# Two cached-attention blocks on one core: the V rows of every fourth pack, their P times V tiles, and where TensorE's loop begins

## The chip, the cores and the metric

The kernel runs on one core of a Trainium2 chip. The metric is the device time of one execution in microseconds (us); lower is better. Of the kernel before there are three timed runs, 747.2, 747.67 and 748.57 us, with a median of 747.67 us, and one profiled execution.

## The reference

Two independent blocks, A and B, each compute the same thing on their own inputs, and the two outputs are joined along the last axis. B is the batch here, H the heads.

```python
B, Sq, D = x.shape            # 16, 64, 640
H, Dh = 32, 128               # k_cache, v_cache: (16, 32, 512, 128), all bf16
q = (x @ wq).reshape(B, Sq, H, Dh).transpose(0, 2, 1, 3)
scores = einsum("bhqd,bhkd->bhqk", q, k_cache) * Dh ** -0.5
p = softmax(scores, axis=-1)
o = einsum("bhqk,bhkd->bhqd", p, v_cache)
return o.transpose(0, 2, 1, 3).reshape(B, Sq, H * Dh) @ wo
```

K and V of both blocks are 268 MB in all, and each byte of them is used once.

## The kernel before

**Packs, turns, phases.** The work is cut into 128 packs, numbered n. A pack is four heads of two batch rows: its K is 1 MB, its V is 1 MB. Four packs (j = n % 4) that share the same two batch rows make a turn, eight turns (all 16 batch rows) make a phase, and there are four phases: the two halves of the heads of block A, then those of block B. A phase has its own quarter of the weights: `wq` through `ws_sb` into `wqp_sb`, and `wo` into `wo_sb`.

**What is done for a pack.** Names are those of the emitters, line numbers those of the profile of before.

- `LDK` (L556, issued by SP): four DMAs of 256 KB into `kn_ring`, six packs deep, in rows of 8 KB.
- `LDV` (L567 or L569, SP): two DMAs of 512 KB into `v_ring`, four packs deep. The load of pack n waits until P times V of pack n - 4 is done.
- `KT` (L621, DVE): the 32 x 32 transposes of K into `kt_ring`, twice per pack.
- `QP` (L607, PE): 20 matmuls for q. `QE` (L613, ACT): q to `qs_ring`.
- `S` (L631, PE): 32 matmuls, the scores into four PSUM banks.
- `EX` (L650, ACT): four exponentials with row sums. `RC` (L663, DVE): reciprocals. `NM` (L679, POOL): four multiplications, P normalised, into `pn_sb`.
- `TR` (L690, PE): 32 transposes of P. `TE` (L700, DVE): two copies to `pT_sb`.
- `PV` (L714, PE): P times V. `OE` (L722, ACT): two copies of the result to `oT_sb`; `ZO` (L726, ACT): a piece of PSUM set to zero.
- `OP` (L734, PE): 8 matmuls with `wo`. After the fourth pack of a turn, `OS` (L744 or L747, DVE) adds to `acc` or `out_sb`, and in phases 1 and 3 `ST` (L753) stores.
- `XT` (L586, PE), once per turn: transposes of x.

**Wide and narrow packs.** There are two layouts of V. In a wide pack a partition of `v_ring` holds 16 consecutive key positions of one head: the DMA moves 128 rows of 4 KB, head i lies in partitions 32 i to 32 i + 31, and `PV` is 128 matmuls on tiles of 32 rows, four such tiles (one per head) next to each other in the array. In a narrow pack a partition holds 8 key positions of each of two heads: the DMA moves 256 rows of 2 KB, and `PV` is 64 matmuls on tiles of 64 rows, two next to each other. `EX` and `NM` lay out P to suit, with the same number of instructions and elements. Before, the packs with j = 0, 1 or 2 are wide and those with j = 3 are narrow (`WIDE = (0, 1, 2)`): 96 wide packs and 32 narrow ones.

**The order of the work.** The table `AT` gives each operation of pack n a due time in units of packs, and each engine runs its list in order of due time. So PE runs, again and again: `QP(n)`, `PV(n-2)`, `S(n)`, `TR(n-1)`, `OP(n-2)`, and once in four packs `XT`. SP's list holds the K and V loads (and some of the weights) in due order; ACT, beside its arithmetic, issues the other weight loads and the stores. Semaphores carry the dependencies.

**TensorE's loop.** All engines but PE run their lists written out. On PE one turn is emitted once, as the body of a loop (L813) that runs 32 times; the pieces ahead of it (one `XT`) and behind it (`PV(126)`, `TR(127)`, `OP(126)`, `PV(127)`, `OP(127)`) are written out. Every matmul is two instructions, a load of the stationary operand (PEld) and the matmul itself; with 821 matmuls, 13 separate waits, 7 subtractions from semaphores and 2 instructions of the loop itself, the body has 1664 instructions. A second, more general version of the program stands behind this one, and is run only if a row sum is out of range; it is not run here.

Of the kernel before, what the change touches and what calls it, by code (L numbers as in the profile page):

```python
# [20 lines left out]
class Cfg:  # L21
# [8 lines left out]
    PERIOD = 4  # L30
    BASE = 32
    KLEAD = 2.5
    WIDE = (0, 1, 2)
    AT = dict(XT=-2.585, XE=-2.383, XC=-0.788, QP=-0.428, QE=-0.224, KT=(-0.672, -0.375), S=0,
              EX=(0.252, 0.307, 0.358, 0.616), RC=(0.572, 0.794), NM=(0.803, 0.854, 1.088, 1.187),
              NMZ=(0.615, 1.231, 1.718, 1.794), TR=1.293, TE=(1.432, 1.47), PV=1.701, OE=(1.888, 2.013), ZO=2.221,
# [396 lines left out]
def mha_kernel(nc, blocks, out, cfg=None):  # L433
    cfg = cfg or Cfg()
# [7 lines left out]
    NBP, NJ = B // 2, 4  # L442
# [2 lines left out]
    assert H % HPH == 0 and NSUB == 2 and cfg.PERIOD == NJ and cfg.NV == NJ  # L445
    NPH = NBLK * NSUB
    NH = NBLK * NBP * H
    WIDE = cfg.WIDE

    plans = []  # L450
    for general in (False, True):
# [5 lines left out]
    with contextlib.ExitStack() as es:  # L457
# [42 lines left out]
        def pack_info(n):  # L500
            g, j = n // NJ, n % NJ
            ph = g // NBP
            return ph // NSUB, g % NBP, j, ph % NSUB * HPH + 4 * j
# [55 lines left out]
        def em_LDV(e, op):  # L559
            n, b = op.idx  # L560
            if n < 0:
                return None, None
            blk, bp, j, h = pack_info(n)
            src = blocks[blk][2][2 * bp + b, h:h + 4]
            dst = v_ring[:, n % NV, b]
            if j in WIDE:
                ins = e.dma_start(dst.rearrange("p t d -> p (t d)"), src.rearrange("h (p t) d -> (h p) (t d)", t=16))  # L567
            else:
                ins = e.dma_start(dst.rearrange("p (a t) d -> p a (t d)", a=2),  # L569
                                  src.rearrange("(a s) (p t) d -> (s p) a (t d)", s=2, t=8))  # L570
            return ins, ins
# [69 lines left out]

        def exp_views(h):
            src, dst = ps[:, h % 4, :], p_ring[:, h % NP, :]
            u = 2 if h // 4 % NJ in WIDE else 4
            return (src.rearrange("q (u t p) -> q t p u", u=u, p=16), dst.rearrange("q (t p u) -> q t p u", p=16, u=u))

        def em_EX(e, op):
            h = op.idx
            src, dst = exp_views(h)
            ins = e.activation(dst, src, ACTF.Exp, scale=1.0, accum_out=rowsum[:, h:h + 1])  # L650
            return ins, ins

        def em_EXG(e, op):
            h = op.idx
            r = h % 4
            src, dst = exp_views(h)
            ins = e.activation(dst, src, ACTF.Exp, bias=negmax[:, r:r + 1], scale=1.0, accum_out=rowsum[:, h:h + 1])
            return ins, ins
# [7 lines left out]
        def em_NM(e, op):  # L666
            h = op.idx
            i = h % 4
            if h < 0:
                ins = e.memset(pn_sb[:, :, :].rearrange("p t c -> p (t c)"), 0.0)  # L670
                return ins, ins
            if h // 4 % NJ in WIDE:
                dst = pn_sb[:, :, 32 * i:32 * i + 32]
                src = p_ring[:, h % NP, :].rearrange("q (t k) -> q t k", t=16)
            else:
                a, s = i // 2, i % 2
                dst = pn_sb[:, 8 * a:8 * a + 8, 64 * s:64 * s + 64]
                src = p_ring[:, h % NP, :].rearrange("q (t k) -> q t k", t=8)
            ins = e.tensor_scalar(dst, src, recip[:, h // 4 % NR, i:i + 1], 1.0, ALU.mult, ALU.mult)  # L679
            return ins, ins  # L680
# [21 lines left out]

        def em_PV(e, op):
            n = op.idx
            wide = n % NJ in WIDE
            tall, tiles, per = (32, 4, 16) if wide else (64, 2, 8)
            first = last = None
            for a in range(4 // tiles):
                for b in range(2):
                    for t in range(per):  # L710
                        for s in range(tiles):
                            rows = slice(tall * s, tall * s + tall)
                            i, c = a * tiles + s, a * per + t
                            last = e.matmul(ps[:, 4 + i, 64 * b:64 * b + 64], v_ring[rows, n % NV, b, c, :],  # L714
                                            pT_sb[rows, b, c, :], start=(t == 0 and i < 2), stop=(t == per - 1),
                                            tile_position=(tall * s, 0), skip_group_check=i >= 2)
                            first = first or last
            return first, last
# [60 lines left out]
        def units(key):  # L779
            return 16 if key[0].startswith("d_") else 1  # L780

        def emit(e, op, p, taken):
            sem = sems[p]
            waits = [(s, v - taken.get(s, 0)) for s, v in op.waits]
            attach = None
            if waits and not op.dma and op.kind not in ("FL1", "WP"):
                attach = waits.pop()
            for s, v in waits:
                e.wait_ge(sem[s], v * units(s))
            kind = "EXG" if p and op.kind == "EX" else op.kind  # L790
            first, last = emitters[kind](e, op)
            if last is None:
                e.sem_inc(sem[op.sem], units(op.sem))
                return
            if attach is not None:
                s, v = attach
                first.wait_op(sem[s], v * units(s), "sem-ge")
            last.then_inc(sem[op.sem], 16 if op.dma else 1)

        def run_program(e, eng, p):  # L800
            progs, counts, loop = plans[p]
            prog = progs[eng]
            if eng != "pe":
                for op in prog:
                    emit(e, op, p, {})
                return
            lo, size, reps, per = loop["lo"], loop["size"], loop["reps"], loop["per"]
            for key in sorted(counts):
                if key[0].startswith("q_"):
                    e.sem_inc(sems[p][key], cfg.BASE)  # L810
            for op in prog[:lo]:
                emit(e, op, p, {})
            with e.Fori(0, reps):  # L813
                taken = {}
                for i, op in enumerate(prog[lo:lo + size]):
                    emit(e, op, p, taken)
                    for s, v in sorted(per.items(), key=str):
                        if loop["take"][s] == i:
                            e.sem_inc(sems[p][s], -v * units(s))
                            taken[s] = v  # L820
            taken = {s: v * reps for s, v in per.items()}
            for op in prog[lo + size * reps:]:
                emit(e, op, p, taken)
# [7 lines left out]
        def run(e, eng):  # L831
            run_program(e, eng, 0)
            e.wait_ge(sems[0][("s_flc_dve",)], 1)
            with e.register("flag_" + eng) as r:
                e.reg_load(r, flag[0:1, 0:1])
                with e.If_ne(r, 128):
                    all_done(e, 0)
                    run_program(e, eng, 1)
                    if eng == "act":
                        all_done(e, 1, ("d_out",))  # L840
            if eng == "act":
                all_done(e, 0, ("d_out",))
# [22 lines left out]
def bass_concat_heads__mha_block_cached__mha_block_cached__near_ridge_kernel(  # L865
    nc: bass.Bass,
    A_x: bass.AP,
    A_k_cache: bass.AP,
    A_v_cache: bass.AP,
    A_wq: bass.AP,  # L870
    A_wo: bass.AP,
    B_x: bass.AP,
    B_k_cache: bass.AP,
    B_v_cache: bass.AP,
    B_wq: bass.AP,
    B_wo: bass.AP,
    out: bass.AP,
):
    blocks = [
        (A_x, A_k_cache, A_v_cache, A_wq, A_wo),  # L880
        (B_x, B_k_cache, B_v_cache, B_wq, B_wo),
    ]
    mha_kernel(nc, blocks, out, Cfg())
# [28 lines left out]
```

## Time and profile before

| | |
|---|---|
| timed runs, us | 747.2, 747.67, 748.57 (median 747.67) |
| profiled execution: span, us | 747.1 |
| what lies around the span | the profile gives no other time of this execution; the median is 0.57 us above its span |
| PE matmul, busy share | 681.3 us, 91% |
| PE weight load | 530.5 us, 71% |
| DVE, ACT, POOL busy | 514.9, 519.7, 404.0 us (69%, 70%, 54%) |
| DMA | 87518 packets, 295.15 MB, mean 395 GB/s |
| mean granted TensorE clock | 0.985 |

The span runs from the first to the last instruction. The engines' shares are averages over stages with different limits. "PE" is the matmul, "PEld" the load of the stationary operand, which overlaps it; SPq is the queue of DMA issues on SP. The DMA share in the tables by window is the time that packets took, divided by the time of 16 DMA engines; it can be over 1, because packets of one engine overlap a little.

### The profile page before, as it was taken

Reading aid. Unit: us, or ns where it says so; the run is one execution under the profiler, and the core shown is the slowest. Engines: PE = TensorE matmul, PEld = TensorE weight load, DVE = VectorE, ACT = ScalarE, POOL = GpSimd, SP = SyncE. Lnnn points to the kernel's source line nnn. Section 1 sums busy time; section 2 is a strip of 40 time slices with the busy share of each in tenths; the row PEclk is TensorE's granted clock in tenths of the full one; section 3 lists DMA queues with packets and bytes.
Section 4 is the critical chain, followed back from the end, with each engine's and each line's share of the span. In section 5 each row is a group of like instructions: output and inputs, shape, how many; then the busy total and the mean of one; then the engine's idle time right before and its main releaser. Section 6 shows DMA issues by size and latency. Waiting matters only on the chain.

```text
span 747.1 us, 57746 instructions
## 1 busy us (share of the span) xinstructions
PE 681.3 (91%) x26518; PEld 530.5 (71%) x26518; DVE 514.9 (69%) x818; ACT 519.7 (70%) x1559; POOL 404.0 (54%) x580
## 2 busy tenths in 40 slices
PE   2779999999999999999988999999997999999994
PEld 2557777777777777777766777777775777777773
DVE  6437777777777677676755676677676677877773
ACT  1438787787777677766756777777775677777772
POOL 3635555655965545545674455455486555555550
PEclk9879999999999999999999999999999999999998
DMA  9999999999999999999999999999999999999970
GB/s 326 391 402 411 412 411 414 411 410 413 405 400 415 411 414 411 412 413 414 410 400 406 410 413 413 412 410 410 413 407 402 410 413 413 413 414 411 410 301 17
DMA packets 87518, 295.15 MB, mean 395 GB/s; under 512 B 13360, under 2 KB 28208, under 8 KB 71088
## 3 DMA queue, kind: packets, MB, share of 16 engines
q1 hardware_dynamic: 76064, 281.43, 94.1%
q10 hardware_dynamic: 11408, 13.27, 5.0%
q14 instruction: 37, 0.30, 0.1%
q8 instruction: 9, 0.15, 0.1%
HBM read 292.03 MB, written 2.62 MB: 394 GB/s over the span
## 4 chain that ended last, share of the span: by engine, by line
SPq 35%; PE 30%; DMA 19%; POOL 5%; issue 4%; ACT 3%; DVE 3%; ACTq 0%; DVEq 0%
SPq L556 23%; PE ps L714 8%; DMA kn_ring<-in_A_k_cache_dram 8%; PE ps L734 7%; PE ps L607 6%; SPq L567 6%; DMA v_ring<-in_B_v_cache_dram 5%; SPq L569 5%; PE ps L631 4%; DMA kn_ring<-in_B_k_cache_dram 4%; PE ps L690 4%; POOL pn_sb L679 4%; DMA ws_sb<-in_A_wq_dram 2%; ACT p_ring L650 2%; ACT oT_sb L722 1%
## 5 line engine op out<-in xcount | busy, mean ns | idle before, releaser
L679 POOL TENSOR_SCALAR pn_sb<-p_ring,recip 128x512 bf16<-128x512 bf16 x508 | 341.8, 692 | 305.5 <-DVE recip L663 305.4
L621 DVE STREAM_TRANSPOSE kt_ring<-kn_ring 128x1024 f32<-128x1024 f32 x256 | 313.5, 1230 | 146.1 <-DMA kn_ring<-in_B_k_cache_dram 103.9
L650 ACT ACTIVATE p_ring<-ps 128x512 bf16<-128x512 f32 x512 | 298.9, 598 | 28.7 <-DMA xn_ring<-in_B_x_dram 6.7
L700 DVE COPY pT_sb<-ps 128x1024 bf16<-128x1024 bf16 x258 | 163.6, 674 | 71.6 <-PE ps L690 68.5
L714 PE MATMUL ps<-pT_sb,v_ring 32*128 32x64 bf16 (+1 forms) x14528 | 163.8, 192 | 26.1 <-DMA v_ring<-in_B_v_cache_dram 11.7
L714 PEld LDWEIGHTS ps<-pT_sb,v_ring 32*128 32x128 bf16 (+1 forms) x14528 | 146.6, 92 | 43.0 <-DMA v_ring<-in_B_v_cache_dram 14.5
L607 PE MATMUL ps<-xT_ring,wqp_sb 128*128 128x128 bf16 x2560 | 166.6, 221 | 7.6 <-POOL xT_ring L596 7.3
L734 PE MATMUL ps<-wo_sb,oT_sb 128*128 128x320 bf16 x1040 | 166.6, 303 | 3.3 <-issue 2.3
L607 PEld LDWEIGHTS ps<-xT_ring,wqp_sb 128*128 128x128 bf16 x2560 | 158.0, 114 | 14.7 <-issue 7.5
L722 ACT ACTIVATE oT_sb<-ps 128x256 bf16<-128x256 f32 x260 | 85.6, 381 | 116.7 <-PE ps L714 116.7
L631 PE MATMUL ps<-kt_ring,qs_ring 32*64 32x512 bf16 x4096 | 139.5, 384 | 0.0
L690 PEld LDWEIGHTS ps<-ident,pn_sb 64*128 64x128 bf16 x4128 | 69.9, 95 | 76.4 <-ACT ps L726 38.4
L613 ACT ACTIVATE qs_ring<-ps 128x512 bf16<-128x512 f32 x128 | 76.5, 598 | 66.6 <-PE ps L607 66.4
L734 PEld LDWEIGHTS ps<-wo_sb,oT_sb 128*128 128x128 bf16 x1040 | 91.9, 98 | 40.9 <-issue 2.5
L650 ACT ACTIVATION_READ_ACCUMULATOR p_ring<-ps 128x1 f32 x512 | 106.0, 207 | 0.0
L690 PE MATMUL ps<-ident,pn_sb 64*128 64x64 bf16 x4128 | 83.8, 191 | 19.6 <-POOL pn_sb L679 9.1
L631 PEld LDWEIGHTS ps<-kt_ring,qs_ring 32*64 32x64 bf16 x4096 | 53.3, 104 | 29.2 <-issue 1.4
L726 ACT ACTIVATE ps<-zeros 128x256 f32<-128x256 bf16 x130 | 51.3, 394 | 0.0
L579 POOL COPY wqp_sb<-ws_sb 128x1280 bf16<-128x1280 bf16 x32 | 39.2, 1255 | 16.4 <-DMA ws_sb<-in_A_wq_dram 16.4
L663 DVE RECIPROCAL recip<-rowsum 128x3 f32<-128x3 f32 (+1 forms) x256 | 36.9, 144 | 3.9 <-ACT p_ring L650 0.6
L596 POOL COPY xT_ring<-xs_sb 128x640 bf16<-128x640 bf16 x32 | 22.9, 716 | 2.0 <-PE ps L607 2.0
L586 PE MATMUL ps<-ident,xn_ring 128*128 128x128 bf16 x165 | 14.9, 222 | 3.3 <-DMA xn_ring<-in_A_x_dram 3.3
(26 smaller groups left out, 65.7 us busy)
## 6 DMA issues: line engine op xcount, KB each, us to landing
kn_ring<-in_A_k_cache_dram SPq DMA_DIRECT2D x256, 256.0 KB
v_ring<-in_A_v_cache_dram SPq DMA_DIRECT2D x128, 512.0 KB, 12.4
kn_ring<-in_B_k_cache_dram SPq DMA_DIRECT2D x256, 256.0 KB
v_ring<-in_B_v_cache_dram SPq DMA_DIRECT2D x128, 512.0 KB, 13.3
ws_sb<-in_B_wq_dram SPq DMA_DIRECT2D x10, 512.0 KB, 16.3
wo_sb<-in_B_wo_dram ACTq DMA_DIRECT2D x8, 640.0 KB, 12.4
ws_sb<-in_A_wq_dram ACTq DMA_DIRECT2D x4, 640.0 KB, 17.4
wo_sb<-in_A_wo_dram SPq DMA_DIRECT2D x4, 640.0 KB, 14.1
```

The costliest lines, as they stand in the source:

```text
L556: ins = e.dma_start(kn_ring[2 * b + l::4, n % NK].rearrange("p a c -> p (a c)"), src)
L607: last = e.matmul(ps[:, 1, f * 128:(f + 1) * 128], w[:, kt, f, :], xT_ring[:, xs, kt, :], start=(kt == 0), stop=(kt == KT - 1))
L613: ins = e.activation(qs_ring[:, op.idx % NQ].rearrange("p f b q -> p (f b q)"), ps[:, 1, :], ACTF.Copy, scale=scale)
L621: ins = e.transpose(dst.rearrange("p c b (h l) -> p c h b l", h=8, l=2), src)
L631: last = e.matmul(ps[64 * b:64 * b + 64, i, :], qs_ring[rows, n % NQ, f, b, :], kt_ring[rows, n % NKT, :, f // 2, b, :, f % 2], start=(f = ...
L650: ins = e.activation(dst, src, ACTF.Exp, scale=1.0, accum_out=rowsum[:, h:h + 1])
L679: ins = e.tensor_scalar(dst, src, recip[:, h // 4 % NR, i:i + 1], 1.0, ALU.mult, ALU.mult)
L690: last = e.transpose(pt_bank(b)[:, 64 * c:64 * c + 64], pn_sb[rows, c, :], ident[rows, rows], tile_position=(64 * b, 0))
L700: ins = e.tensor_copy(pT_sb[:, b].rearrange("p t q -> p (t q)"), pt_bank(b))
L714: last = e.matmul(ps[:, 4 + i, 64 * b:64 * b + 64], v_ring[rows, n % NV, b, c, :], pT_sb[rows, b, c, :], start=(t == 0 and i < 2), stop=(t ...
L722: ins = e.activation(oT_sb[:, 2 * a:2 * a + 2, :], o_ps[:, 2 * a:2 * a + 2, :], ACTF.Copy)
L734: last = e.matmul(out_ps[:, s, :], oT_sb[:, i, :], wo_sb[:, 4 * j + i, s * NH0:(s + 1) * NH0], start=(j == 0 and i == 0), stop=(j == NJ - ...
```

## The change

A pack is now wide unless it is one of the last two: `wide(n)` is true for n below 126. So 126 packs are wide and 2 (126 and 127) narrow: thirty-one packs go from narrow to wide, and pack 126 goes from wide to narrow. The same test picks the layout in the load of V, in `EX`, `NM` and `PV`. The body of TensorE's loop gets 64 more matmuls and so 128 more instructions, 1792 in all. The loop is now made on PE alone with `nc.Fori(..., head_slot={e.engine: 0})`: the loader is asked to place the loop's first instruction at instruction slot 0 of a fetch block of 256 instructions, with a branch over the slots left unused ahead of it. The lists of SP, ACT, DVE and POOL, with their waits, are the same.

```diff
-    WIDE = (0, 1, 2)
+    NARROW = 2
...
-    WIDE = cfg.WIDE
+    NPACK = NH // 4
+
+    def wide(n):
+        return n < NPACK - cfg.NARROW
...
-            if j in WIDE:
+            if wide(n):
                 ins = e.dma_start(dst.rearrange("p t d -> p (t d)"), src.rearrange("h (p t) d -> (h p) (t d)", t=16))
...
-            u = 2 if h // 4 % NJ in WIDE else 4
+            u = 2 if wide(h // 4) else 4
...
-            if h // 4 % NJ in WIDE:
+            if wide(h // 4):
                 dst = pn_sb[:, :, 32 * i:32 * i + 32]
...
-            wide = n % NJ in WIDE
-            tall, tiles, per = (32, 4, 16) if wide else (64, 2, 8)
+            tall, tiles, per = (32, 4, 16) if wide(n) else (64, 2, 8)
...
-            with e.Fori(0, reps):
+            with nc.Fori(0, reps, engines=[e.engine], head_slot={e.engine: 0}):
```

## The prediction

> **What bounds the kernel now.** I read the page first: the slices and the DMA summary.
>
> ```profile
> PE 681.3 (91%) x26518; PEld 530.5 (71%) x26518; DVE 514.9 (69%) x818; ACT 519.7 (70%) x1559; POOL 404.0 (54%) x580
> ...
> DMA  9999999999999999999999999999999999999970
> GB/s 326 391 402 411 412 411 414 411 410 413 405 400 415 411 414 411 412 413 414 410 400 406 410 413 413 412 410 410 413 407 402 410 413 413 413 414 411 410 301 17
> DMA packets 87518, 295.15 MB, mean 395 GB/s; under 512 B 13360, under 2 KB 28208, under 8 KB 71088
> ...
> q8 instruction: 9, 0.15, 0.1%
> ```
>
> The DMA engines are busy in every slice but the last two, at 400 to 415 GB/s from the third on: one unbroken stream that ends near 731 us. PE, at 91%, stands close behind. Which leads, and where, is told by the length of a turn, taken between two `XT` in the trace. Six turns of phase 0 (from 73 us) and three of phase 3 take 20.71 us, to the hundredth; those of phases 1 and 2 take 21.2 to 22.7 us, and 24.4 to 26.0 us around a change of weights. The waits say why: over the span, and then SP's own in 77.46 to 160.3 us and in 560 to 660 us:
>
> ```profile
> DVE kt_ring L621 <- DMA kn_ring<-in_B_k_cache_dram: 103.9, 64, 4.0
> DVE kt_ring L621 <- DMA kn_ring<-in_A_k_cache_dram: 42.0, 27, 2.8
> ```
>
> ```profile
> SPq L567 <- PE ps L714: 18.5, 12, 1.9
> ```
>
> ```profile
> SPq L567 <- PE ps L714: 0.6, 1, 0.6
> ```
>
> Early, SP waits for `PV` to free a V buffer and nobody waits for DMA: the arithmetic paces the turn, at 20.71 us. Later SP hardly waits, and DVE waits for K. The semaphores of V say the same: V lands 6 to 7 us before its `PV` in phase 0, and within 1.1 us of it from pack 34 to pack 125. In phase 3 both limits nearly meet.
>
> What makes 20.71 is a chain over two packs, `EX`, `NM`, `TR`, `OP`, `QP`, `PV`, `S`, `EX`. PE's timeline from 97.9 us, a narrow `PV` and what follows it:
>
> ```profile
> 100.86 1.11 PE L714 MATMUL ps<-pT_sb,v_ring 64*128 64x64 bf16 x64
> 101.89 1.07 PE L631 MATMUL ps<-kt_ring,qs_ring 32*64 32x512 bf16 x32
> 103.15 0.64 PE L690 MATMUL ps<-ident,pn_sb 64*128 64x64 bf16 x32 [0.19 <-POOL pn_sb L679]
> ```
>
> `TR` waits here for POOL, which ran since 100.32 us on an `EX` that began at 98.17: the narrow `PV` is not on the chain.
>
> The end and the first turn show what code costs. PE's timeline from 728 us, the granted clock there, and the first turn's chain:
>
> ```profile
> 732.84 0.52 PE L690 MATMUL ps<-ident,pn_sb 64*128 64x64 bf16 x23 [0.79 <-ACT oT_sb L722]
> 734.63 0.44 PE L690 MATMUL ps<-ident,pn_sb 64*128 64x64 bf16 x9 [1.27 <-issue]
> 735.00 2.32 PE L734 MATMUL ps<-wo_sb,oT_sb 128*128 128x320 bf16 x8
> 737.25 1.42 PE L714 MATMUL ps<-pT_sb,v_ring 64*128 64x64 bf16 x64
> ```
>
> ```profile
> 734.60:738.00 3.40, 3.37 (x47) 2.08 (x49) 2.82 (x8) 0.00 (x0) 0.00 (x0) 0.50 0.02 5
> ```
>
> ```profile
> 32.13 2.80 issue
> ...
> 38.84 2.26 issue
> ...
> 45.82 3.07 issue
> ```
>
> The three "issue" stalls stand exactly 256 PE instructions apart, each beside a 16 KB packet on the instruction queue q8: PE has run out of code and waits for a block of 256. Counting on in both directions, the loop begins at slot 80 of a block and ends at slot 208 of the sixth after it: seven blocks, with an eighth fetched ahead at 52.7 us. Then q8 is silent until 731.9 us, so these eight blocks stay through 31 back edges (each branch takes 208 ns). The ninth comes 304 instructions behind the loop, inside `TR(127)`: the 1.27 us stall. PE then runs at half clock (column 0.50) for 3.4 us, and `OP(126)` takes 2.25 us instead of 1.2.
>
> **The change, part by part.**
>
> *V in longer rows.* Thirty packs fewer load V in 512 packets of 2 KB, and do it in 256 of 4 KB: per DMA engine 16 pairs become 16 packets. In the trace's DMA packets a 2 KB one takes 87.2 ns (mean of 16384), a 4 KB one 162.6, an 8 KB one 315.3: two of the short ones take 11.9 ns more than one of 4 KB. But packets overlap (the DMA share in windows is 1.02 to 1.03), so that is the upper bound. A fit of the packets counted in windows of 1 to 5 us to 16 engines' full time gives 7.2 to 9.4 ns for the difference; I take 8. Then 30 x 16 x 8 ns = 3.8 us off the stream; the bounds are 5.7 us (11.9 ns) and 0, if the bytes alone set the rate. In phase 0 the gain is banked as lead, since V waits 12 to 13 us in the DMA queue and the queue does not run dry; in phases 1 and 2 each turn gains 0.13 us. In phase 3 it is capped by the arithmetic: its last six whole turns sum to 125.4 us, and 6 x 20.71 = 124.3, so they can give 1.1 us, and 6 x 0.13 = 0.8 is asked for. For the packs behind them I take a little off: 3.7 us.
>
> The Trainium skill (DMA: Bandwidth & Descriptors, "Why small descriptors are slow (HBM only)") gives a fixed cost of about 3 cycles per packet and 32 bytes of descriptor. At its 850 MHz and 32 bytes per cycle that makes an estimate of 4.7 ns per packet saved and 2.3 us in all; the sum would be 742.7 us. The fit's 7.2 to 9.4 ns stand above it, and the measurement decides.
>
> *64 matmuls more per turn.* A wide `PV` issues in 1.03 us (median of 87), a narrow one in 0.92: 0.11 us more per turn. After a narrow `PV` the gap from `S` to `TR` is 0.53 us, after wide ones 0.30 to 0.41; the least is 0.30, so 0.23 us of POOL's time hide the 0.11. Cost: 0. Without that cover it is 0.11 us in some 13 turns paced by arithmetic, 1.4 us, of which only phase 3's 0.8 reach the end. `EX` and `NM` take the same in both layouts (four `NM` 2.69 us in each). No wait is added or moved; SP issues the same two DMAs per pack.
>
> *The loop's head.* 1664 + 128 = 1792 instructions are seven blocks exactly. From slot 80 they would reach into an eighth, and a ninth would be fetched ahead; from slot 0 it stays seven and one ahead, as many as are held now. Steady cost: 0. In the first turn the blocks' edges move, but the DMA stream is full from 5 us on and V waits 11 to 17 us there: 0 either way, with at most one stall (3 us) of PE's time under that cover.
>
> *The end.* The last turn is paced by arithmetic. `PV(126)` narrow saves 0.11 us. Behind the loop a block's edge now comes after 256 instructions instead of 48 and 304, within `PV(127)`; before, the fetch took some 3.4 us from the block entered to the code run, and from the loop's exit to `PV(127)` there are over 4 us. So `TR(127)` runs through (0.64 us), `TE` follows (1.3 us), `OP(126)` lies beside it, and `PV(127)` starts at about 734.8 instead of 737.25 us; without the half clock it ends 0.25 us sooner still. In all 2.7 us off; bounds 0.1 (stall and half clock stay) and 2.8. The rest, from `OP(127)` to the end, is unchanged.
>
> Sum: 747.1 - 3.7 - 2.7 = 740.7 us of span. The median of the runs lies 0.57 us above the profiled span: 741.3 us.
>
> **The rivals.**
>
> *The arithmetic takes the place.* If the wider `PV` does reach the two-pack chain, phase 3 gains nothing from DMA (0.8 back) and pays 0.8: 742.9 us. Against it is the 0.23 us of cover; for it, that phase 3 has no other slack.
>
> *The end keeps its stall,* because the fetch comes late again or the clock falls anyway: 2.6 us back, 743.9 us. For it: `PV(127)` still waits for `TE`, so PE idles and the clock may drop.
>
> *Rows change nothing,* the stream being bound by bytes: only the end gains, 744.9 us. For it: the rate is 410 to 414 GB/s with every mix. Against it: the fit, in which the difference is several times its error.
>
> *The loop does not stay in PE's memory,* slower. The price is in the first turn: 2.26 to 3.07 us for a block fetched too late, 2.7 in the mean. One block per turn, 31 turns: 84 us. In some 16 turns of phases 1 and 2 PE has about 1.4 us to spare (22.1 against 20.71), which hides 22: 741.3 + 62 = 803 us. It decides if a ninth block is fetched before the branch goes back: the branch now stands in the last slot of its block, where before 48 slots were left, or the head is not placed as asked. Against it: eight blocks held through 31 turns before, and eight needed now. A harder form, all seven blocks fetched in each turn, would cost 7 x 84 = 588 us; since nothing of it shows before, it gets 0.01 of this rival's chance.
>
> The Trainium skill (Runtime: NRT & Kernel Launch, "Instruction fetch mechanics") says that a taken branch to a block outside a window of two makes the engine wait for a fetch; that speaks for this rival's harder form. The trace disagrees for PE: 31 branches six blocks back, no packet on q8. The same section gives PE room for 2048 instructions, eight such blocks, and with that the trace agrees.
>
> **How the numbers follow.** My forecast has a chance of 0.57, the arithmetic 0.13, the end 0.12, rows 0.06, the loop 0.10, and 0.02 is left for no difference. The range goes from 739.2 (5.5 us from rows and 2.8 at the end make 739.4, and 0.2 are scatter) to 744.9 and leaves out the loop. A measurement of this kernel tells about 0.2%, 1.5 us, from no change; all cases but the loop's lie beyond that on the fast side: faster 0.88, same 0.02, slower 0.10.
>
> **What would show it.** Right: about 7700 fewer DMA packets; turns of phases 1 and 2 shorter by some 0.13 us; those of phase 0 still 20.71 us; no packet on q8 between the first and the last turn; no "issue" stall in the last `TR`, and `OP(126)` at 1.2 us. Wrong: q8 packets in every turn, turns above 20.8 us in phase 0, or a stream that ends as late as before.

## The result and the profile after

The changed kernel takes 743.03 us (median of four runs, 742.91 to 743.14), the kernel before 747.43 us (four runs, 746.59 to 748.57). The ratio is 0.9938, with a 95% interval of 0.9926 to 0.9951: faster by 4.4 us. A second set of six runs, beside eleven of the kernel before, gives 743.31 us and a ratio of 0.9943 (0.9931 to 0.9954). The profiled execution has a span of 741.4 us and a time of 743.14.

Engines, DMA summary and the instruction queue, from the page of after:

```profile
PE 680.6 (92%) x28502; PEld 532.2 (72%) x28502; DVE 517.0 (70%) x818; ACT 519.8 (70%) x1559; POOL 405.0 (55%) x580
...
DMA  9999999999999999999999999999999999999980
...
DMA packets 79841, 295.19 MB, mean 398 GB/s; under 512 B 13360, under 2 KB 28208, under 8 KB 63408
...
q8 instruction: 10, 0.16, 0.1%
```

There are 7677 DMA packets fewer and 1984 matmuls more, and the DMA engines are still busy in every slice but the last two. Between 53.5 and 727.8 us the trace has no packet on q8: the longer loop stays where it is.

The waits of DVE for K over the span, and SP's own waits for P times V in the two windows used before (77.46 to 160.3 us, then 560 to 660 us):

```profile
DVE kt_ring L624 <- DMA kn_ring<-in_B_k_cache_dram: 69.7, 40, 3.7
DVE kt_ring L624 <- DMA kn_ring<-in_A_k_cache_dram: 35.1, 25, 2.9
```

```profile
SPq L570 <- PE ps L716: 28.2, 16, 1.9
```

```profile
SPq L570 <- PE ps L716: 11.6, 13, 1.3
```

DVE waits 104.8 us for K where it waited 145.9. In the late window SP now waits for `PV` 13 times, where it did so once: the loads have a lead in phase 3 that they did not have.

PE's timeline of after in phase 0, a `PV` of a fourth pack, which is now wide:

```profile
100.84 1.21 PE L716 MATMUL ps<-pT_sb,v_ring 32*128 32x64 bf16 x128
101.98 1.07 PE L634 MATMUL ps<-kt_ring,qs_ring 32*64 32x512 bf16 x32
103.14 0.64 PE L693 MATMUL ps<-ident,pn_sb 64*128 64x64 bf16 x32
```

The wait of `TR` for POOL (0.19 us before) is gone, and `TR` starts no later behind `PV`: 2.30 us after its start, 2.29 before.

The end, on PE's timeline of after, and the granted clock there (the column before the last two):

```profile
727.91 1.11 PE L716 MATMUL ps<-pT_sb,v_ring 64*128 64x64 bf16 x64 [0.28 <-DVE pT_sb L703]
729.77 0.64 PE L693 MATMUL ps<-ident,pn_sb 64*128 64x64 bf16 x32 [0.75 <-ACT oT_sb L724]
730.34 1.26 PE L736 MATMUL ps<-wo_sb,oT_sb 128*128 128x320 bf16 x8
731.88 1.11 PE L716 MATMUL ps<-pT_sb,v_ring 64*128 64x64 bf16 x64 [0.28 <-DVE pT_sb L703]
734.03 1.26 PE L736 MATMUL ps<-wo_sb,oT_sb 128*128 128x320 bf16 x8 [1.03 <-ACT ps L728]
```

```profile
732.00:736.00 4.00, 2.35 (x73) 1.65 (x69) 2.43 (x8) 0.94 (x3) 0.00 (x0) 1.00 0.02 4
```

`TR(127)` is one piece of 32, no "issue" stall follows, `OP(126)` takes 1.26 us where it took 2.32, and the clock is whole.

Where the 5.7 us of span went, from the starts of `XT` in the two traces:

| | before | after | difference |
|---|---|---|---|
| whole turns of phase 0, us each | 20.71 | 20.72 to 20.74 | +0.02 |
| start of the last six whole turns | 594.33 | 590.78 | -3.55 |
| these six turns, sum | 125.43 | 126.05 | +0.62 |
| last `XT` to the end of the span | 27.4 | 24.6 | -2.8 |

So phases 0 to 2 and the first turns of phase 3 gain 3.55 us, the end gains 2.8, and between them 0.62 is given back. That last term has the wrong sign for the forecast, and most of the experiments are about it.

### The profile page after: what moved, and what is told of

Read it like the earlier page. It is cut to its first block, busy times and chain, and to the rows that moved or that the text cites. A ratio compares the mean times of both kernels' runs of the same rounds, so it can differ in the third digit from the quotient of the medians.

```text
span 741.4 us, 61715 instructions
## 1 busy us (share of the span) xinstructions
PE 680.6 (92%) x28502; PEld 532.2 (72%) x28502; DVE 517.0 (70%) x818; ACT 519.8 (70%) x1559; POOL 405.0 (55%) x580
## 4 chain that ended last, share of the span: by engine, by line
PE 45%; SPq 38%; DMA 7%; issue 4%; ACT 3%; POOL 2%; DVE 1%; ACTq 0%; DVEq 0%
SPq L559 24%; SPq L570 12%; PE ps L716 11%; PE ps L736 11%; PE ps L610 10%; PE ps L634 7%; PE ps L693 6%; DMA v_ring<-in_B_v_cache_dram 3%; DMA ws_sb<-in_A_wq_dram 2%; DMA kn_ring<-in_B_k_cache_dram 2%; ACT oT_sb L724 2%; SPq L544 1%; POOL pn_sb L682 1%; ACT ps L728 1%; POOL wqp_sb L582 1%
## 5 line engine op out<-in xcount | busy, mean ns | idle before, releaser
L716 PE MATMUL ps<-pT_sb,v_ring 32*128 32x64 bf16 x16512 | 164.5, 192 | 18.6 <-DMA v_ring<-in_B_v_cache_dram 11.6
L716 PEld LDWEIGHTS ps<-pT_sb,v_ring 32*128 32x128 bf16 x16512 | 148.6, 91 | 34.0 <-DMA v_ring<-in_B_v_cache_dram 14.4
```

## The experiments

Each ratio is to the kernel before, run in the same rounds, with its 95% interval. "Held" is a `PV` in whose weight loads, as the trace has them, one starts over 45 ns behind the one before; in a wide `PV` they usually start 8 or 9 ns apart. The length of a hold is what the `PV` takes, from its first weight load to its last, over the usual 1.017 us.

**1. The head alone.** Before, with one line changed.

```diff
-            with e.Fori(0, reps):
+            with nc.Fori(0, reps, engines=[e.engine], head_slot={e.engine: 0}):
```

> The kernel before with one edit: TensorE's loop (still 1664 instructions, three wide packs and one narrow one per turn) begins at slot 0 of a block. Theory A (the gain at the end comes from where the code blocks end): block edges behind the loop come after 128 and 384 instructions, inside PV(126) and PV(127), so the last TR has no issue stall and OP(126) runs at full clock: span 2.4 to 2.7 us below before, all of it behind the last turn; turns unchanged (20.71 us in phase 0). Rival B (the end gained because packs 126 and 127 are both narrow, not by the edges): within 0.3 us of before, with the stall still there or moved.

Measured: 746.22 us, ratio 0.9979 (0.997 to 0.9988). The turns of phase 0 take 20.73 or 20.74 us, and the last `XT` stands at 719.74 us, 0.02 from before's: the gain, 2.5 us of span, is all behind it, as theory A has it. The end of PE's timeline:

```profile
732.83 0.64 PE L690 MATMUL ps<-ident,pn_sb 64*128 64x64 bf16 x32 [0.79 <-ACT oT_sb L722]
733.40 1.26 PE L734 MATMUL ps<-wo_sb,oT_sb 128*128 128x320 bf16 x8
734.95 1.11 PE L714 MATMUL ps<-pT_sb,v_ring 64*128 64x64 bf16 x64 [0.28 <-DVE pT_sb L700]
```

The stall and the half clock are gone, and `PV(127)` starts 2.3 us sooner than in before's profile. By medians the gain is only 1.5 us. The 23 runs of before beside it spread from 746.41 to 749.39 us, those of this kernel from 745.79 to 746.54: before's end has a cost that differs from run to run, and its profiled execution had much of it. The next experiment but one shows a milder case of it.

**2. The longer loop without the head.** After, with `e.Fori(0, reps)` put back, so that 1792 instructions begin at about slot 80.

> The kernel after without the head's placement: 1792 instructions from slot 80 or so, which touch eight blocks, with a ninth next. Theory A (TensorE's memory holds eight blocks, and entering the last one fetches the ninth): instruction packets on q8 in every turn, at least one issue stall of 2 to 3 us per turn, 31 x 2.7 = 84 us less about 20 hidden in phases 1 and 2: 800 us or more, and up to 1300 us if all blocks are fetched again. Rival B (there is room for nine blocks): no packets on q8 between the first and the last turn, 743 to 746 us, the stall at the end in another place.

Measured: 1362.54 us, ratio 1.8253 (1.8188 to 1.8318). The page's instruction queue, the waits of PE for "issue", and the chain from 610 us:

```profile
q8 instruction: 288, 4.72, 1.5%
```

```profile
PEld ps L610 <- issue: 196.9, 32, 7.5
PE ps L610 <- issue: 177.8, 31, 6.8
```

```profile
610.87 1.00 issue
611.88 0.99 PE ps L736 x6
612.87 1.12 PE ps L610 x20
613.98 0.92 PE ps L716 x101
614.91 3.35 issue
```

288 packets are nine in each of 32 turns, where before had nine in the whole run. The 619.5 us more than after, over 31 turns that go back, are 20.0 us per turn, 2.2 us for each of nine blocks. That is not the price of the fetches alone: the mean granted clock is 0.82 here and 0.99 in after. The DMA engines are busy for only 0.63 of the time between 200 and 1200 us. One block more than the loop can have costs not one fetch per turn but all of them. The rest of the change stands on that one argument of the loop.

**3. The rows alone.** Before, with the test in the load of V changed; `PV`, `EX` and `NM` stay as they were.

```diff
-            if j in WIDE:
+            if n < 126:
```

> The kernel before with the 4 KB rows alone: V of the packs below 126 comes in 4 KB rows, everything else as before (so P times V of every fourth pack takes V from the wrong places). Theory A (the rows are worth 3.7 to 4.5 us of the DMA stream, and the wide PV takes back what is lost in phase 3): span 4 to 5 us below before, the turns of phase 3 at 20.71 us or a little above, the stall at the end as before. Rival B (phase 3 loses for another reason, such as the loads themselves): 2.5 to 3.5 us below before, with turns of 20.9 to 21.3 us in phase 3.

Measured: 745.58 us, ratio 0.9972 (0.9961 to 0.9984). The last six whole turns sum to 126.12 us though every fourth `PV` is still narrow: the loss in phase 3 comes without the wider `PV`, as rival B has it for the turns (20.74 to 21.42 us here). The stall in `TR(127)` is there, but 0.69 us long and with no half clock behind it, so the size of this end does differ between executions:

```profile
731.88 0.32 PE L690 MATMUL ps<-ident,pn_sb 64*128 64x64 bf16 x9 [0.69 <-issue]
732.13 1.26 PE L734 MATMUL ps<-wo_sb,oT_sb 128*128 128x320 bf16 x8
```

**4. Rows and head.** Experiments 1 and 3 together; against after it lacks only the 64 matmuls per turn.

> The 4 KB rows and the loop's head at slot 0, but PV, EX and NM as before (P times V of every fourth pack takes V from the wrong places): the kernel after without the 64 more matmuls per turn. Theory A (the wide PV costs 1 to 1.6 us in phase 3, where TensorE has no other slack and a PV of 128 matmuls takes 1.17 instead of 1.03 us): 1 to 1.6 us below the kernel after, phase 3's turns at 20.71 us. Rival B (the wide PV is free): the same as after within 0.5 us, and phase 3's turns at 20.9 to 21.3 us here too.

Measured: 743.61 us, ratio 0.9947 (0.9931 to 0.9962). The six turns sum to 126.50 us. After, with the wide `PV` in every pack, is not slower. The wider `PV` costs nothing that these runs can tell, and what phase 3 gives back is not its doing.

**5. All packs narrow.** Before, with `WIDE = ()`.

> The kernel before with every pack narrow: 96 packs more load V in rows of 2 KB, and every PV is 64 matmuls. Theory A (a 4 KB row in place of two of 2 KB saves 8 ns or somewhat more on each DMA engine, 0.13 to 0.18 us per pack): 12 to 17 us above before, all in turns that DMA paces, and no PV above 0.92 us. Rival B (bytes alone set the rate): within 3 us of before. Rival C (the rows cost less than the fit says, and fewer matmuls give PE slack): 3 to 8 us above.

Measured: 758.95 us, ratio 1.0144 (1.0125 to 1.0163). 96 packs more with rows of 2 KB cost 10.88 us by the times. But the body is shorter here (1280 instructions), so the blocks' edges behind the loop move too: `TR(127)` is one piece of 32, with no stall, and the end takes 24.6 us from the last `XT` as in after, where before's takes 27.4. Up to the last `XT` (732.69 us, 719.76 in before) the rows cost 12.9 us: 0.135 us per pack, or 8.4 ns for each of the 16 pairs that a DMA engine moves. For the thirty packs of the change that makes 4.0 us. The cost of the rows is theory A's; the time falls short of its 12 us because the end is shorter.

**6. Which wait is attached to `PV`.** After, with the separate wait of `PV` and the attached one exchanged.

```diff
             attach = None
+            if op.kind == "PV":
+                waits.sort(key=lambda w: w[0][0] != "d_v")
```

> The kernel after with the two waits of PV changed round on TensorE: the separate wait is now that for V, the one on the first instruction that for TE. Theory A (a wide PV is held up for 0.14 to 0.2 us when a DMA issue on SP ends within it): the same as after, 742.5 to 743.5 us, with the held PVs of phase 3 as they were. Rival B (a wide PV is held up because TensorE's sequencer, waiting for TE, starts to feed it too late): phase 3's PVs at 1.03 us, 0.5 to 1.5 us below after.

Measured: 742.95 us, ratio 0.9931 (0.9917 to 0.9945), after's time. The six turns sum to 126.55 us: the order of the waits is not it.

**7. V in four DMAs of 64 partitions.** After, with each DMA of V cut into halves by partition.

```diff
-            dst = v_ring[:, n % NV, b]
+            dst = v_ring[rows, n % NV, b]
...
+                              src[2 * u:2 * u + 2].rearrange("h (p t) d -> (h p) (t d)", t=16))
```

> The kernel after with each V load in two halves of 64 partitions: four DMA issues of 256 KB per pack in place of two of 512 KB, with the same rows. Theory A (the end of a DMA issue holds up a wide PV): issues now run on into the next PV also where they did not before, so wide PVs above 1.1 us appear in phase 0, whose turns rise above 20.73 us by 0.1 to 0.5 us, and 1 to 4 us are lost in all. Rival B (the holding up has to do with the data on its way, not the issues): PVs as in after, within 0.7 us of it.

Measured: 1197.68 us (1169.56 to 1240.74), ratio 1.5708 (1.5648 to 1.5769). The one profile, at 1226.8 us of span, is of a longer run than the median. Its DMA lines:

```profile
DMA  9999999999999999999999999999999999999993
...
DMA packets 83939, 295.22 MB, mean 241 GB/s; under 512 B 17456, under 2 KB 32304, under 8 KB 67504
...
q8 instruction: 10, 0.16, 0.1%
```

The code stays put, and the DMA engines are as busy as ever, but at 241 GB/s for 398: a packet of 4 KB takes 283 ns where after's takes 162, and one of 8 KB, the size of K's, 524 for 315. For the held `PV` it says nothing, since the transfers set the pace everywhere; it says that the two 512 KB DMAs over all 128 partitions are worth keeping. Number, size and partitions of V's DMAs change together here, and no run tells them apart.

**8. V in one DMA per pack.** After, with both batch rows in one DMA of 1 MB, and for that all packs wide (`NARROW = 0`).

> The kernel after with the V of a pack in one DMA of 1 MB, one issue in place of two, and all 128 packs wide (so the block's edge behind the loop falls at the start of TR(127)). Theory A (the end of a DMA issue holds up a wide PV): a sixth fewer issues, fewer PVs above 1.1 us, turns 0.3 to 1 us shorter in all up to the last one; the end loses 0.7 to 1.5 us to a stall in TR(127). Rival B: the turns up to the last one as in after, within 0.3 us.

Measured: 746.65 us, ratio 0.9978 (0.9968 to 0.9988). From pack 8 on, 44 of its wide `PV` have the issue of a K DMA ending in them (from 0.1 us behind the first weight load to 0.25 ahead of the last), and 42 of these are held, with a mean of 1.17 us for the 44 where 1.02 is the rule. The six turns sum to 125.89 us, and the last `XT` stands at 716.70 us, 716.83 in after: rival B. What was taken away here are issues of V, and the paragraph on the traces below shows that these hold nothing up. What it loses to after is at the end:

```profile
727.77 1.20 PE L713 MATMUL ps<-pT_sb,v_ring 32*128 32x64 bf16 x127 [0.28 <-DVE pT_sb L700]
731.25 0.21 PE L713 MATMUL ps<-pT_sb,v_ring 32*128 32x64 bf16 x1 [2.27 <-issue]
732.21 1.03 PE L690 MATMUL ps<-ident,pn_sb 64*128 64x64 bf16 x32 [0.75 <-ACT oT_sb L721]
733.17 2.32 PE L733 MATMUL ps<-wo_sb,oT_sb 128*128 128x320 bf16 x8
```

A wide `PV(126)` has 256 instructions and fills the block behind the loop to its edge; its last matmul waits 2.27 us for code, and a half clock follows (0.50 granted from 731.25 to 735.5 us). That is what the narrow `PV(126)` of the change avoids.

**What the traces then suggested.** In five traces (before, after, experiments 1, 3 and 4), from pack 8 on, 146 of 478 wide `PV` are held, mostly for 0.13 to 0.23 us, and the hold is over some 385 ns behind the end of a DMA issue on SP. It is K's issues alone. Each of the 146 has one ending from 0.1 us behind its first weight load to 0.25 ahead of its last, and only 8 others have; of the 324 without, none is held, though 87 have an issue of V ending there. In all traces but those of experiments 2 and 7, again from pack 8 on, a K issue that ended at least 0.15 us behind the start of a wide `PV`, and at least 0.385 ahead of its last weight load, was followed by a gap 506 times in 507, one of V never in 158; and of 107 K issues that ended in its first 0.1 us none was. What sets K's DMAs apart (256 KB in rows of 8 KB into every fourth partition; V's are 512 KB or more over all 128) no run separates. PE and SP of after in phase 3, a `PV` and what follows it, and the issues of K and V around it (start, length):

```profile
666.22 1.35 PE L716 MATMUL ps<-pT_sb,v_ring 32*128 32x64 bf16 x128
667.49 1.07 PE L634 MATMUL ps<-kt_ring,qs_ring 32*64 32x512 bf16 x32
668.50 0.64 PE L693 MATMUL ps<-ident,pn_sb 64*128 64x64 bf16 x32
```

```profile
663.17 3.25 SPq L559 DMA_DIRECT2D kn_ring<-in_B_k_cache_dram  x4
667.64 0.81 SPq L570 DMA_DIRECT2D v_ring<-in_B_v_cache_dram  x2
```

The last K issue ends at 666.42 us, 0.2 behind the start of that `PV`, which takes 1.35 us instead of 1.21. In phase 0 the four K issues take 2.39 us and end 0.3 us or more ahead of the next `PV`. An issue of V that ends in a `PV`, in phase 2 (PE, then SP):

```profile
433.87 1.21 PE L716 MATMUL ps<-pT_sb,v_ring 32*128 32x64 bf16 x128
```

```profile
432.37 1.84 SPq L570 DMA_DIRECT2D v_ring<-in_B_v_cache_dram  x2
434.25 1.22 SPq L559 DMA_DIRECT2D kn_ring<-in_B_k_cache_dram  x1
```

It ends at 434.21 us, 0.34 behind the start, and the `PV` takes its 1.21 us. The next two runs bring ends of K issues into `PV` on purpose.

**9. K's issues moved onto `PV`.** After, with one more wait on SP.

```diff
+    for n in range(7, N):
+        at[("LDK", (n, 0))].deps.append(at[("OP", n - 7)])
```

> After, with one more wait: SP issues the four K DMAs of pack n only once OP(n-7) is done, which is 1.1 to 1.3 us ahead of the next P times V; their four issues (0.6 us each) then end about 0.6 us before, at, and 0.6 and 1.2 us behind the start of that P times V, in phase 0 too, where none ends in one now. Theory A (the end of a DMA issue on SP holds TensorE up for a while some 0.4 us later, which shows in wide P times V, where TensorE uses its instructions fastest): nearly every wide P times V of phase 0 is held for 0.13 to 0.4 us; it is a link of the two-pack chain, so the turns of phase 0 go from 20.73 to 21.2 to 22.2 us, and those of the last part of phase 3 likewise. The DMA stream, with 12 us of lead in its queue, makes up for phase 0, so the time goes up by little: 743.5 to 747 us. Theory B (the held P times V have another cause, and the issue's end beside them is chance): in phase 0 wide P times V stay at 1.03 us and the turns at 20.73, and the time is 743.0 us.

Measured: 745.02 us, ratio 0.9964 (0.9951 to 0.9976). PE, then SP, in phase 0:

```profile
102.46 1.46 PE L719 MATMUL ps<-pT_sb,v_ring 32*128 32x64 bf16 x128
103.85 1.07 PE L637 MATMUL ps<-kt_ring,qs_ring 32*64 32x512 bf16 x32
104.85 0.64 PE L696 MATMUL ps<-ident,pn_sb 64*128 64x64 bf16 x32
```

```profile
101.44 2.39 SPq L562 DMA_DIRECT2D kn_ring<-in_A_k_cache_dram  x4
```

Every `PV` of phase 0 from pack 8 on is held, for 0.13 to 0.26 us, and the turn goes from 20.73 to 21.34 to 21.40 us. No engine waits for K or V in these turns (80 to 160 us), so it is not that K comes later. Theory A holds for K's issues: when SP makes them slows PE by 0.6 us per turn, with nothing else of PE's work or waits changed.

**10. The same wait in the kernel before,** where wide and narrow `PV` stand side by side.

> Before, with the same wait of the K DMAs on OP(n-7). Here wide (j = 0, 1, 2) and narrow (j = 3) P times V stand side by side in one run. Theory A with its second half (TensorE's queue of instructions covers the pause unless it is emptied at 4 ns per instruction; a narrow P times V uses 7 ns): in phase 0 the wide ones are held, the narrow ones stay at 0.89 to 0.92 us; turns of 21.1 to 21.8 us for 20.71. Without that half, the narrow ones are held as well, for 0.1 to 0.4 us. Theory B: neither is held, turns 20.71. Time by A 748 to 751 us, by B 747.4.

Measured: 747.76 us, ratio 1.0001 (0.999 to 1.0011). Two `PV` that follow each other in phase 0:

```profile
97.53 1.46 PE L717 MATMUL ps<-pT_sb,v_ring 32*128 32x64 bf16 x128
...
102.81 1.11 PE L717 MATMUL ps<-pT_sb,v_ring 64*128 64x64 bf16 x64
```

The wide ones are held and the turn is 21.21 to 21.29 us for 20.71, which is theory A again. The total does not move and stays below theory A's 748 us, since in before the DMA stream makes up for phase 0, and phase 3 has no lead. The narrow ones keep their 1.11 us, but for theory A's second half this is no test: in phase 0 the K issues end 0.10 and 0.73 us behind the start of a narrow `PV`. At 0.10 wide ones are not held either, and 0.73 and 0.385 are more than a narrow `PV` takes from its first weight load to its last (0.89). Experiment 5 tests it: of 47 K issues that ended 0.15 to 0.50 us behind the start of a narrow `PV`, one was followed by a gap; in wide `PV`, over the traces with such, 214 of 214 were. So narrow `PV` are not held. That PE's store of instructions runs dry because a wide `PV` uses one in 4 ns and a narrow one in 7 is the likely reading, but argued: no row shows that store.

**11. One K issue moved into the second half of `PV`.** After, as an attempt to get phase 3's 0.62 us back.

```diff
+    for n in range(7, N):
+        at[("LDK", (n, 3))].deps.append(at[("QP", n - 4)])
```

> After, with the last of the four K DMAs of pack n issued only once QP(n-4) is done, so that its issue (0.6 us) ends some 0.7 us behind the start of P times V, and the other three are over before it. If what phase 3 gives back is the issues that end in wide P times V, then few of those are held there (after: three in four of packs 99 to 110), the last six whole turns of phase 3 sum to 124.3 to 125.2 us for after's 126.05, and the time is 0.3 to 1.5 us below after's. Rival: the long turns of phase 3 come from elsewhere (late K, DMA), the held P times V being a bystander: the sum stays near 126 and the time at after's, 743.0. If the last issue ends early enough to hold P times V itself, phase 0 shows it: turns over 20.8 us.

Measured: 744.34 us, ratio 0.9957 (0.9945 to 0.9968); slower than after beside it. The issue ended some 0.6 us into `PV` and held its tail, in phase 0 too: turns of 21.01 to 21.07 us, and a sum of 126.44 in phase 3. This is the third outcome that its expectation names, so it does not decide whether phase 3 would get faster without such ends.

**12. After once more,** in the same rounds as experiment 11.

> The changed kernel itself, on the same chip and in the same rounds as the one beside it, since the two may lie within 0.2%: 742.9 to 743.2 us, phase 0 turns of 20.73 us, the last six whole turns of phase 3 at about 126.0 us.

Measured: 743.31 us (742.90 to 744.09), ratio 0.9943 (0.9931 to 0.9954). The six turns sum to 125.99 us, and one by one they agree with the first trace within 0.07 us. No version that was run beats after by more than these runs can tell.

## Why the prediction was right, and where its sum was off

**Direction and range.** The forecast was 741.3 us, the result 743.03: inside the range and on the expected side, with 1.7 us between them. Two steps make up the difference: the distance from span to time with 1.1 us, the rows with 0.8; the end gave 0.1 more than was asked of it.

**From the span to the time.** The prediction added 0.57 us, the distance from before's profiled span to the median of its runs. In every run that gave both, time is 1.7 to 1.9 us above the span of the same execution. By that, an estimate, the profiled execution of before took about 748.8 us and was one of the slower ones. The forecast span of 740.7 us would have been a time of 742.4.

**Rows, -3.7.** Up to the last six whole turns the size was right: 3.55 us, and 8.4 ns per pair by experiment 5 where 8 was taken. The Trainium skill (DMA: Bandwidth & Descriptors, "Why small descriptors are slow (HBM only)") led to an estimate of 4.7 ns and 2.3 us; experiment 5 stands above it, and the measurement decides. Rows alone gained 2.17 us by medians, but that is what is left after phase 3 has given some back. The step that failed is the cap for phase 3: "they can give 1.1 us", with 0.8 asked for. The six turns lost 0.62 instead. The lead that the rows bring lets SP's issues of K slide over `PV`, and a held wide `PV` is a link of the two-pack chain.

**The size of that.** In phase 0 of experiment 11 a hold of 0.16 us in each `PV` lengthens the turn by 0.31 us; in experiment 9, 0.22 us lengthen it by 0.64. So about the first 0.08 us of a hold are covered and the rest counts (4 x 0.08 = 0.32 for the one, 4 x 0.14 = 0.56 for the other). Summed in that way over the six turns, the holds of after are worth 0.96 us and those of before 0.14. The 0.82 between them is near the 0.62 lost.

Late K is not the cause: DVE waits for it 0.6 us in the first of after's six turns and not at all in the others, where in before it waits 4.4 to 5.8 us in each. And the fourth of the six turns differs between runs by its holds: 20.71 us in before and in experiment 8, which have none there, 20.86 in after (0.13 us of holds in all), 21.00 in experiment 11 (0.58) and 21.28 in experiment 9 (0.80). So holds lengthen turns in phase 3 too. That they are the whole of the 0.62 is argued, since no run took them all away. The third turn takes 21.00 us in before without a hold and 21.01 in after with 0.44 us of them, and before's second, 20.99, has none either, so something else is there too, and it stays open.

**64 matmuls more per turn, 0.** Right: 20.73 us for 20.71 in phase 0, and experiment 4, which lacks them, is not faster than after. The cover is used up, though. Of the 0.23 us of POOL's time 0.13 were taken by the longer `PV` (1.02 for 0.89 us between first and last weight load), and the 0.08 us that a hold may last unseen is near what is left.

**The loop's head, 0.** Right, for the reason given: seven blocks and one ahead fit.

**The end, -2.7.** Right against the profiled execution, with 2.8. Against the median it is 1.5 (experiment 1), because before's profile had the longer stall and the half clock, and other executions have less of it.

**The rivals.** "The arithmetic takes the place" named 742.9 us, which is near the result, but by another way: its mechanism, the wider `PV` on the chain, is refuted by experiment 4. "The end keeps its stall" and "rows change nothing" fell with experiments 1 and 3. "The loop does not stay" is what experiment 2 shows where the head is missing, and in the form that had been given almost no chance: not one block per turn for 803 us, but all of them. It came to 2.2 us per block, at the lower clock, where 2.7 were priced. It was weighed down with the argument that nothing of it showed before, where eight blocks were needed and eight fit; that said nothing of nine.

## What to carry to other kernels

Before a loop is lengthened, count the instruction blocks that it touches from the slot where it begins: here the step from eight to nine cost 620 us, and one argument for the place of the loop's head avoided it. When a stream that set the pace gets faster, the engine that leads next sees its other neighbours at new moments; here the issues of K's loads moved onto the densest matmuls, which is the likely reason that 0.6 of 3.5 us were lost again. Add an edit's gain to the time of the same execution that was read, and look at how far the runs of the kernel before scatter, since a profile may have caught a slow one.

## What the hardware showed that was not expected

- The end of a K issue on SP (256 KB in rows of 8 KB) holds up TensorE in dense small matmuls: gaps that end some 385 ns behind it, 0.13 to 0.26 us per `PV` of 128 matmuls in phase 0 of experiment 9. Issues of V (512 KB) do not (none of 158), and a `PV` of 64 matmuls is not held (46 of 47 in experiment 5).
- A loop of TensorE that needs one block more than eight fetches all nine in every turn (288 packets for 9): 20.0 us per turn, 2.2 us for each block, at a granted clock of 0.82 and with the DMA engines 0.63 busy.
- V in four DMAs of 256 KB over 64 partitions each, with the same rows of 4 KB, instead of two of 512 KB over 128, brings the whole stream from 398 to 241 GB/s; K's own packets slow down with them (8 KB in 524 ns for 315).
